# Attention ahead of two MLP layers on one core: the first half's maxima three tiles apart, two weight-conversion steps behind the next first unit, reciprocals ahead of the loads

## The chip, the cores and the metric

The kernel runs on one core of one Trainium2 chip. TensorE (PE; its weight loads are PEld) multiplies, VectorE (DVE), ScalarE (ACT) and GpSimd (POOL) do the elementwise work, and SyncE (SP) issues most of the DMAs, in the order of the program. The metric is the device time of one execution in microseconds (us); less is better.

## The reference

```python
def _attn_ref(q, k, v):                 # 4 x 8 heads, 1152 x 64
    q_pool = q.reshape(B, H, S // 2, 2, D).mean(axis=3)
    scores = scale * np.matmul(q_pool, k.transpose(0, 1, 3, 2))
    scores = scores - np.max(scores, axis=-1, keepdims=True)
    attn = np.exp(scores)
    attn = attn / (np.sum(attn, axis=-1, keepdims=True) + 1e-09)
    return np.matmul(attn, v)
# x: 2304 tokens x 512; then h = x @ w_in (2048 wide), g = h - tanh(h), x = g @ w_out,
# and the same again with g = h * sigmoid(1.702 h) and other weights.
```

## The kernel before

**Pairs and halves.** Attention takes the 32 heads two at a time, as 16 pairs; a pair has 576 pooled queries and is worked off in two halves of 288 queries. The loop `for h in range(NH)` runs over the 32 halves; even halves are a pair's first, odd ones its second. The program writes every engine's order out by hand (`todo[h]`, and the lists filled by `at(h, place, job)` and run by `do(h, place)`); no scheduler moves anything.

**What a half holds.** Nine score tiles S (`scores`, line 429: three matmul steps with high and low parts of q and k, and a fourth that adds the row of negated maxima, `row`), each followed by an exponential on ACT (L435). Between them stand "units" X (`unit`, L359, L351 for unit 6, called R here) that compute the maxima of the *next* pair, each ended by a DVE reduction (L371) out of PSUM, and in even halves the two "corner" units C (L366) of the pair itself. Then come the products with v (`products`, L480) and the sums over ones (L493). In an even half the order is given by `usual[0]`, in an odd one by `usual[1]`, where units 4 to 8 of the next pair stand; unit 4 is the first non-S of an odd half.

**PSUM.** All of these tiles come from one pool of four buffers, handed out in turn: a tile can start when the reader of the tile four before it is done.

**The row of maxima.** When unit 6 (R) of the next pair is reduced, `max_rows` and `send_rows(p + 1, 0)` put the maxima into a row with six small DMAs of SP (L388, `row<-tt`). The first S of the next even half needs that row in its fourth step.

**The sums' way.** `sums` (SP, L514) sends the sums of the pair before to DVE's layout, `recip` adds and inverts them (DVE L522, L523) and writes them to DRAM (SP, L525, `rd<-r`), `spread` reads them back broadcast (SP, L531, `rbd<-rd`), and `normalise` multiplies (DVE, L540). `recip` stands at the end of the even half, `spread` at the start of the odd one; on SP, `spread` stands ahead of the six row DMAs.

**Weights of the first layer** are converted along the way, each piece over four halves: `shift` (ACT L142 and DVE L143), `sign` (DVE L149), `flush` (DVE L156), `tail` (DVE L163), then `split` (ACT L170, POOL L171). `shift` and `flush` stand at the end of an even half, ahead of `recip`.

**Loads.** By their shapes `load_k` and `load_v` move 576 KB each, `load_sum` and `fetch_low` 288 KB each, and the two of `spread` 288 KB together. `load_k` (L290) is the first thing on SP in an even half, ahead of `sums`; `load_v` (L294) and `load_sum` (L285) stand in the place "load", after the last unit. `fetch_low` (L342, `ql<-qd`) is the first thing on SP in an odd half.

**POOL** adds the first probabilities of a half (L446), three in a row and one more after a DVE addition (`rest`, L464), and computes `kl` (L328), which is told to wait for the last DVE instruction noted in `last["v"]` (`recip`'s or `normalise`'s).

Of the kernel before, what the change touches and what calls it, by code (L numbers as in the profile page):

```python
# [7 lines left out]
F32 = mybir.dt.float32  # L8
F32R = mybir.dt.float32r
I32 = mybir.dt.int32  # L10
AF = mybir.ActivationFunctionType
# [12 lines left out]
def f32(ap):  # L24
    return ap.bitcast(F32)
# [3 lines left out]
def tile_pooled_attention_two_moe(  # L29
# [11 lines left out]
    nc = tc.nc  # L41
# [92 lines left out]
    def convert_steps(raw, hi, lo, shape, box, eng=None):  # L134
        def shift():
            box["t"] = wpool.tile([128, DM], I32, tag="wt", name="wt", bufs=2)
            if raw.dtype == F32:
                nc.scalar.activation(f32(box["t"][:]), raw, AF.Copy)
                return
            top = raw[:, :, 1]  # L140
            box["a"] = wpool.tile([128, DM], F32, tag="wa", name="wa", bufs=1)
            nc.scalar.activation(box["a"], f32(top), AF.Abs)  # L142
            nc.vector.tensor_scalar(  # L143
                out=box["t"], in0=top, scalar1=3, scalar2=0x3FFFFFF8,
                op0=ALU.logical_shift_left, op1=ALU.bitwise_and,
            )

        def sign():
            nc.vector.scalar_tensor_tensor(  # L149
                out=box["t"], in0=raw[:, :, 1], scalar=-0x40000000, in1=box["t"],  # L150
                op0=ALU.bitwise_and, op1=ALU.bitwise_or,
            )

        def flush():
            t, a = box["t"], box["a"]
            nc.vector.scalar_tensor_tensor(  # L156
                out=f32(t[:]), in0=a, scalar=2.0 ** -15 * 1.125, in1=f32(t[:]),
                op0=ALU.is_ge, op1=ALU.mult,
            )

        def tail():
            t = box["t"]
            nc.vector.scalar_tensor_tensor(  # L163
                out=t, in0=raw[:, :, 0], scalar=29, in1=t,
                op0=ALU.logical_shift_right, op1=ALU.bitwise_or,
            )

        def split():
            t = f32(box["t"][:]).rearrange("p (a b) -> p a b", a=shape)
            nc.scalar.activation(hi, t, AF.Copy)  # L170
            job = (eng or nc.gpsimd).tensor_tensor(lo, t, f32(hi), op=ALU.subtract)  # L171
            if eng is None:
                after(job, last.pop("rest", None))

        def nothing():
            pass

        bits = [sign, flush, tail] if raw.dtype == I32 else [nothing] * 3
        return [shift, *bits, split]

# [38 lines left out]
    def attention(ctx: ExitStack):  # L219
# [124 lines left out]
        def unit(p, n):  # L344
            d = pairs[p]
            mx = ps.tile([128, 2, 512], F32, tag="ps", name="mx")
            a = n - 9
            if n == 6:
                for j in range(4):
                    for s, r in enumerate(sides):  # L350
                        nc.tensor.matmul(  # L351
                            mx[:, s, KN * j:KN * j + KN], d["qh"][r, 128 * j:128 * j + 128],
                            d["kh"][r, 2 * 512:], start=True, stop=True)
                out = d["mt"][:, 20:28].rearrange("p (j s) -> p j s", j=4)
                src = mx.rearrange("p s (j k) -> p j s k", j=4)
            elif n < 9:
                j, c = divmod(n if n < 6 else n - 1, 2)
                for s, r in enumerate(sides):
                    nc.tensor.matmul(  # L359
                        mx[:, s, :], d["qh"][r, 128 * j:128 * j + 128],  # L360
                        d["kh"][r, 512 * c:512 * c + 512], start=True, stop=True)
                out, src = d["mt"][:, 10 * c + 2 * j:10 * c + 2 * j + 2], mx
            else:
                for h in range(2):
                    for s, r in enumerate(sides):
                        nc.tensor.matmul(  # L366
                            mx[:, s, 0:HB], d["cq"][r, (1 - h) * QL:(3 - h) * QL],
                            d["kh"][r, h * SP + a * HB:h * SP + a * HB + HB],
                            start=(h == 0), stop=(h == 1))
                out, src = d["mt"][:, 8 + 10 * a:10 + 10 * a], mx[:, :, 0:HB]  # L370
            nc.vector.tensor_reduce(out, src, AX.X, ALU.max, negate=True)  # L371
# [174 lines left out]
        def at(h, when, fn, *args):  # L546
            jobs.setdefault((h, when), []).append(lambda: fn(*args))
# [2 lines left out]
            for job in jobs.pop((h, when), ()):  # L550
                job()

        usual = "S C S C S S X S S S X S S X X", "S X S S S X S R S S S X S X"
        begin = "S X S S S X S C S S S C S X X", "S X S S S X S S X S X S S R X X"
        NH = 2 * NPAIR
        todo, ahead = {}, {}
# [19 lines left out]
        for n, (kind, f) in enumerate(order):  # L576
            ld, shift, *more, split = piece(kind, f)
            mine = slots_at[4 * n:4 * n + 4]
            at(mine[0] - 1, "load", ld)
            at(mine[0], "pre" if mine[0] % 2 else "end", shift)  # L580
            for h, job in zip(mine[1:], more, strict=True):
                at(*((h, "end") if h < NH - 2 else (NH - 1, "pre")), job)
            at(mine[-1] + 1, "pre" if mine[-1] + 1 < NH - 1 else "end", split)
        for c in range(NKC):
            at(NH - 2, "pre", split_high, 0, c)
# [2 lines left out]
        for p in range(NPAIR):  # L588
            h = 2 * p
            if p > 0:  # L590
                at(h - 2, "load", load_v, p)
                if p == 1:
                    at(h - 2, "pre", prep_corner, p)
                    at(h - 2, "end", prep_ql, p)
                    at(h - 2, "pool", prep_kl, p, 0)
                    at(h - 1, "end", prep_kl, p, 1, nc.vector)
                else:
                    at(h - 2, "pool", prep_kl, p, 0)
                    at(h - 1, "pool", prep_kl, p, 1)
                    at(h - 1, "first", fetch_low, p, "ql")  # L600
                at(h, "start", sums, p - 1)
                at(h, "pre" if h == NH - 2 else "end", recip, p - 1)
                at(h + 1, "start", spread, p - 1)
                at(h + 1, "end", normalise, p - 1)
            if p > 1:
                at(h - 4, "start", new_pair, p)
                at(max(h - 6, 0), "start", load_one, p)
                at(max(h - 6, 0), "gp" if p > 2 else "start", load_other, p)
                at(h - 4, "load", load_sum, p)
                at(h - 4, "first", load_k, p)  # L610
                at(h - 3, "pre", prep_qh, p)
                at(h - 3, "pre", prep_corner, p)
                at(h - 3, "pre", minus_qh, p)
                at(h - 3, "pre", prep_kh, p, 0)
                at(h - 3, "pre", prep_kh, p, 1)
                at(h - 3, "gp", take_qh, p)
# [51 lines left out]
        for h in range(NH):  # L668
            p, x = divmod(h, 2)
            do(h, "first")  # L670
            do(h, "start")
            g = h * KT
            t = 0
            late = [t for g in rest_of(p, x) for t in g[1:]] if h < NH - 1 else []
            for u in todo[h]:
                if u is None:
                    scores(g + t)
                    if h < NH - 1 and t < KADD - full(p, x) or t < 4:
                        add(p, x, t)
                    elif h == NH - 1 and t in (5, 7):  # L680
                        add_two(p, x, t)
                    t += 1
                    if t == KT and late and h != 1:
                        add_rest(p, x, late.pop(0))
                    continue
                unit(*u)
                if u == (p + 1, 6):
                    max_rows(p + 1, 0)
                    send_rows(p + 1, 0)
                if u == (p, 10):  # L690
                    max_rows(p, 1)
                    send_rows(p, 1)
                if t == KT and late:
                    add_rest(p, x, late.pop(0))
                    if late and x == 0 and full(p, x):
                        add_rest(p, x, late.pop(0))
                        end_rows(p)
            while late:
                add_rest(p, x, late.pop(0))
            if h == NH - 2:  # L700
                end_rows(p)
            do(h, "load")
            do(h, "pre")
            do(h, "gp")
            products(p, x)
            if x == 0 and not full(p, x):
                end_rows(p)
            do(h, "end")
            do(h, "pool")
# [652 lines left out]
```

## Time and profile before

| | us |
|---|---|
| median of three runs | 1176.01 |
| the three runs | 1171.54, 1176.01, 1176.41 |
| the profiled execution, own time | 1176.05 |
| its span in the profile | 1174.3 |
| attention in the span | about 0 to 392 |
| PE busy / DVE busy / ACT busy / POOL busy | 1161.6 / 992.5 / 652.9 / 453.6 |

The span is that of the trace; the execution's own time has 1.75 us more around it. PE counts as busy from a matmul's modelled start to its end, so a share of 99% does not say that PE is never held up; that is read from the chain and from the distances between equal pieces of work.

### The profile page before, as it was taken

Reading aid. Unit: us, or ns where it says so; the run is one execution under the profiler, and the core shown is the slowest. Engines: PE = TensorE matmul, PEld = TensorE weight load, DVE = VectorE, ACT = ScalarE, POOL = GpSimd, SP = SyncE. Lnnn points to the kernel's source line nnn. Section 1 sums busy time; section 2 is a strip of 40 time slices with the busy share of each in tenths; the row PEclk is TensorE's granted clock in tenths of the full one; section 3 lists DMA queues with packets and bytes.
Section 4 is the critical chain, followed back from the end, with each engine's and each line's share of the span. In section 5 each row is a group of like instructions: output and inputs, shape, how many; then the busy total and the mean of one; then the engine's idle time right before and its main releaser. Section 6 shows DMA issues by size and latency. Waiting matters only on the chain.

```text
span 1174.3 us, 23203 instructions
## 1 busy us (share of the span) xinstructions
PE 1161.6 (99%) x9260; PEld 971.5 (83%) x9260; DVE 992.5 (85%) x1242; ACT 652.9 (56%) x969; POOL 453.6 (39%) x321
## 2 busy tenths in 40 slices
PE   9999999999999999999999999999999999999998
PEld 7767676767777888888898898898889999999996
DVE  6888988878988799999999999998986899886442
ACT  4667566656665678676666666655654333342220
POOL 7667676766766223333232333221000222222211
PEclk9999999999999999999999999999999999999999
DMA  6455655555542021111111111112998757765512
GB/s 191 123 118 137 162 127 133 146 143 130 125 111 62 12 64 36 55 54 37 54 36 54 37 36 36 37 54 95 389 389 311 275 215 287 269 225 206 206 54 90
DMA packets 58221, 156.29 MB, mean 133 GB/s; under 512 B 14080, under 2 KB 19712, under 8 KB 58112
## 3 DMA queue, kind: packets, MB, share of 16 engines
q1 hardware_dynamic: 53536, 146.14, 35.8%
q0 software_dynamic: 4032, 8.26, 4.9%
q8 instruction: 73, 1.20, 0.4%
q10 hardware_dynamic: 544, 0.39, 0.1%
q14 instruction: 36, 0.29, 0.1%
HBM read 124.39 MB, written 33.69 MB: 135 GB/s over the span
## 4 chain that ended last, share of the span: by engine, by line
PE 77%; DVE 14%; ACT 4%; issue 2%; DMA 1%; POOL 1%; SPq 1%; DVEq 0%; ACTq 0%; POOLq 0%
PE sc L429 13%; PE y L1048 13%; PE y L1236 12%; PE h L1139 11%; PE acc L480 11%; PE b L996 5%; PE a L996 3%; PE c L996 3%; PE mx L359 3%; DVE work L1182 2%; DVE work L1199 2%; DVE wt L149 2%; DVE wt L143 1%; ACT work L1180 1%; PE acc L493 1%
## 5 line engine op out<-in xcount | busy, mean ns | idle before, releaser
L371 DVE TENSOR_REDUCE mt<-mx 128x2 fp32r<-128x1024 f32 (+2 forms) x176 | 198.1, 1136 | 41.0 <-PE mx L359 22.1
L435 ACT ACTIVATE pf<-sc 128x576 f32<-128x576 f32 x288 | 173.8, 655 | 24.2 <-PE sc L429 15.1
L1236 PE MATMUL y<-mem,big 128*128 128x512 f32 (+1 forms) x780 | 185.1, 368 | 1.2 <-POOL mem L1153 1.2
L1236 PEld LDWEIGHTS y<-mem,big 128*128 128x128 f32 x780 | 142.6, 188 | 21.2 <-POOL mem L1153 2.3
L1034 POOL TENSOR_TENSOR mem<-work,mem 128x768 fp32r<-128x768 f32 x24 | 46.2, 1938 | 289.4 <-ACT mem L1029 274.4
L446 POOL TENSOR_TENSOR sum<-sum,pf 128x576 f32<-128x576 f32 x95 | 137.4, 1446 | 29.2 <-DVE rest L464 23.9
L480 PE MATMUL acc<-pf,v 128*32 128x288 f32 x2304 | 146.3, 407 | 0.0
L1139 PE MATMUL h<-mem,big 128*128 128x512 f32 (+1 forms) x564 | 127.1, 377 | 0.0
L480 PEld LDWEIGHTS acc<-pf,v 128*32 128x32 f32 x2304 | 71.6, 110 | 65.6 <-ACT pf L435 5.0
L1139 PEld LDWEIGHTS h<-mem,big 128*128 128x128 f32 x564 | 104.4, 188 | 17.0
L1153 POOL TENSOR_TENSOR mem<-work,mem 128x1024 fp32r<-128x1024 f32 (+1 forms) x40 | 89.1, 2227 | 75.9 <-ACT mem L1151 75.9
L1048 PE MATMUL y<-big,mem 128*128 128x512 f32 x405 | 114.0, 390 | 0.0
L1201 ACT ACTIVATE work<-work 128x1024 f32<-128x1024 f32 (+1 forms) x40 | 39.1, 977 | 107.5 <-DVE work L1199 107.5
L429 PE MATMUL sc<-qh,kh 64*128 64x288 f32 x576 | 94.0, 315 | 0.0
L171 POOL TENSOR_TENSOR big<-wt,big 128x512 fp32r<-128x512 f32 x25 | 32.6, 1302 | 155.5 <-ACT big L170 142.5
L429 PE MATMUL sc<-row,sel 64*128 64x288 f32 x576 | 88.5, 293 | 3.9 <-DMA row<-tt 2.4
L1048 PEld LDWEIGHTS y<-big,mem 128*128 128x128 f32 x405 | 76.0, 188 | 15.5
L429 PE MATMUL sc<-qh,kl 64*128 64x288 f32 x576 | 87.5, 293 | 0.0
L429 PE MATMUL sc<-ql,kh 64*128 64x288 f32 x576 | 87.2, 292 | 0.0
L1139 PE MATMUL h<-mem,w 128*128 128x512 f32 (+1 forms) x376 | 84.7, 377 | 0.0
L501 ACT ACTIVATE u<-acc 128x576 f32<-128x576 f32 x30 | 19.6, 653 | 107.3 <-PE acc L493 107.3
L1139 PEld LDWEIGHTS h<-mem,w 128*128 128x128 f32 x376 | 69.6, 188 | 11.3
(176 smaller groups left out, 2580.5 us busy)
## 6 DMA issues: line engine op xcount, KB each, us to landing
mem<-x SPq DMA_DIRECT2D x36, 768.0 KB
big<-x SPq DMA_DIRECT2D x27, 768.0 KB
raw<-in_moe_w_in_dram SPq DMA_DIRECT2D x32, 512.0 KB
raw<-in_moe_w_out_dram SPq DMA_DIRECT2D x32, 512.0 KB
v<-in_v_dram SPq DMA_DIRECT2D x16, 576.0 KB
x<-big SPq DMA_DIRECT2D x12, 768.0 KB
kr<-in_k_dram SPq DMA_DIRECT2D x15, 576.0 KB
rbd<-rd SPq DMA_DIRECT2D x32, 144.0 KB
```

The costliest lines, as they stand in the source:

```text
L371: nc.vector.tensor_reduce(out, src, AX.X, ALU.max, negate=True)
L429: nc.tensor.matmul(sc[:, s, 0:HB], w[r], m[r, xs], start=(n == 0), stop=(n == 3))
L435: nc.scalar.activation(pf, sc[:, :, 0:HB], AF.Exp, scale=SCALE)
L446: job = nc.gpsimd.tensor_add(out, parts[p, x], new)
L480: nc.tensor.matmul(acc[32 * n:32 * n + 32, 0], pairs[p]["v"][:, s, t, 32 * h:32 * h + 32], new[t][:, s, :], start=(t == 0), stop=(t == KT ...
L996: nc.tensor.matmul(bank[nm][:, fp, 0:G], w[:, wo, a, 128 * c:128 * c + 128], x[:, b, c, :], start=(k == 0), stop=(k == 5))
L1034: eng.tensor_tensor(g[:, :, 1], halves[n][:, fp], f32(g[:, :, 0]), op=ALU.subtract)
L1048: nc.tensor.matmul(y, gts[2 * side + fp][:, j, r, 128 * t:128 * t + 128], wo[:, p, :], start=(k == 0), stop=(k == len(terms) - 1))
L1139: nc.tensor.matmul(hb[:, j, 0:TBS[b]], wi[:, c, w, :], x[r][c], start=(k == 0), stop=(k == 3 * NKC - 1))
L1153: eng.tensor_tensor(gt[:, :, 1, :], g, f32(gt[:, :, 0, :]), op=ALU.subtract)
L1201: nc.scalar.activation(a, u, AF.Relu, bias=-T2)
L1236: nc.tensor.matmul(ys[m][:, 0:w], lhsT, rhs, start=(fp == 0 and not low and j == p == 0), stop=(fp == 1 and low and j == 1))
```

## The change

The two C units of an even half stand together behind the first S, and the X units come after 3, 6 and 9 score tiles (and one more) where they came after 4, 7 and 9. `shift` and `flush` move from the end of an even half to a new place "mid" in the odd half after it, just behind unit 4 and its reduction; ACT's `Abs` moves from `shift` to `sign`, which stands at the end of an odd half. `recip`, with its SP write, moves from the end of an even half to a new place "rows", behind `end_rows`, which is between the reductions of the last two X units and, on SP, ahead of the loads. `load_k` moves from the head of the even half to the place "load".

```diff
         def shift():
             ...
-            box["a"] = wpool.tile([128, DM], F32, tag="wa", name="wa", bufs=1)
-            nc.scalar.activation(box["a"], f32(top), AF.Abs)
             nc.vector.tensor_scalar(...)
         def sign():
+            box["a"] = wpool.tile([128, DM], F32, tag="wa", name="wa", bufs=1)
+            nc.scalar.activation(box["a"], f32(raw[:, :, 1]), AF.Abs)
             nc.vector.scalar_tensor_tensor(...)
...
-        usual = "S C S C S S X S S S X S S X X", "S X S S S X S R S S S X S X"
+        usual = "S C C S S X S S S X S S S X X", "S X S S S X S R S S S X S X"
...
-            at(mine[0], "pre" if mine[0] % 2 else "end", shift)
+            at(*((mine[0], "end") if mine[0] == NH - 2 else (mine[0] + 1, "mid")), shift)
             for h, job in zip(mine[1:], more, strict=True):
-                at(*((h, "end") if h < NH - 2 else (NH - 1, "pre")), job)
+                if h >= NH - 2:
+                    at(NH - 1, "pre", job)
+                elif h % 2:
+                    at(h, "end", job)
+                else:
+                    at(h + 1, "mid", job)
...
-                at(h, "pre" if h == NH - 2 else "end", recip, p - 1)
+                at(h, "pre" if h == NH - 2 else "rows", recip, p - 1)
...
-                at(h - 4, "first", load_k, p)
+                at(h - 4, "load", load_k, p)
...
                 unit(*u)
+                if u == (p + 1, 4):
+                    do(h, "mid")
...
                         end_rows(p)
+                        do(h, "rows")
```

## Rows read from the trace of the kernel before

**Rows 1.** The page, part 1: busy us, share of the span, instructions.
```profile
PE 1161.6 (99%) x9260; PEld 971.5 (83%) x9260; DVE 992.5 (85%) x1242; ACT 652.9 (56%) x969; POOL 453.6 (39%) x321
```
**Rows 2.** Chain in order of time (start, length): first score tiles of odd halves.
```profile
75.03 0.73 PE sc L429 x8
...
99.72 0.73 PE sc L429 x8
...
123.02 0.73 PE sc L429 x8
...
169.49 0.73 PE sc L429 x8
...
193.40 0.73 PE sc L429 x8
...
239.91 0.73 PE sc L429 x8
...
266.75 0.72 PE sc L429 x8
```
**Rows 3.** The same chain, where it runs through a row DMA.
```profile
250.71 2.92 DMA row<-tt
```
**Rows 4.** Windows: busy us by engine, then granted clock, DMA share, GB/s.
```profile
252.00:254.00 2.00, 0.41 (x5) 0.32 (x5) 0.08 (x1) 0.22 (x1) 1.39 (x1) 1.00 0.39 70
254.00:256.00 2.00, 2.00 (x21) 2.00 (x22) 0.76 (x1) 0.87 (x2) 0.00 (x0) 0.53 0.66 194
```
**Rows 5.** SP's queue in order of time (start, length), in three odd halves.
```profile
128.68 3.29 SPq L388 DMA_DIRECT2D row<-tt  x6
...
176.07 3.36 SPq L388 DMA_DIRECT2D row<-tt  x6
...
246.21 2.15 SPq L531 DMA_DIRECT2D rbd<-rd  x2
248.45 3.29 SPq L388 DMA_DIRECT2D row<-tt  x6
```
**Rows 6.** Waits, 60 to 385 us: total us, times, longest.
```profile
SPq L290 <- POOL kl L328: 43.7, 12, 4.6
SPq L531 <- DMA rd<-r: 32.8, 14, 4.6
...
PEld mx L359 <- DVE mt L371: 4.8, 13, 0.4
```
**Rows 7.** DVE in order of time, an even half into the next odd.
```profile
158.83 1.56 DVE L371 TENSOR_REDUCE mt<-mx 128x2 fp32r<-128x576 f32 x2 [0.46 <-PE mx L366]
...
163.87 1.41 DVE L464 TENSOR_TENSOR rest<-pf 128x576 f32<-128x576 f32 x1
...
168.43 1.21 DVE L371 TENSOR_REDUCE mt<-mx 128x2 fp32r<-128x1024 f32 x1
169.56 0.68 DVE L156 SCALAR_TENSOR_TENSOR wt<-wa,wt 128x512 f32<-128x512 f32 x1
170.16 0.18 DVE L522 TENSOR_REDUCE r<-s 128x9 f32<-128x27 f32 x1
170.37 0.22 DVE L523 RECIPROCAL r<-r 128x9 f32<-128x9 f32 x1
170.50 1.22 DVE L371 TENSOR_REDUCE mt<-mx 128x2 fp32r<-128x1024 f32 x1
172.31 2.36 DVE L371 TENSOR_REDUCE mt<-mx 128x2 fp32r<-128x1024 f32 x2 [0.59 <-PE mx L359]
```
**Rows 8.** POOL in order of time, three places.
```profile
163.24 1.42 POOL L446 TENSOR_TENSOR sum<-sum,pf 128x576 f32<-128x576 f32 x1
...
192.35 1.27 POOL L171 TENSOR_TENSOR w<-wt,w 128x512 fp32r<-128x512 f32 x1 [1.62 <-DVE rest L464]
...
269.14 1.43 POOL L446 TENSOR_TENSOR sum<-pf 128x576 f32<-128x576 f32 x1 [0.43 <-ACT pf L435]
```
**Rows 9.** DVE's reduction of unit 4 in the half of the last row above.
```profile
267.76 1.23 DVE L371 TENSOR_REDUCE mt<-mx 128x2 fp32r<-128x1024 f32 x1 [0.56 <-PE mx L359]
```

## The prediction

> **What bounds the kernel now.** I read the page first, then the chain, then the queues that feed it. PE is busy for 1161.6 of 1174.3 us [rows 1], so the reader is to see that only time in which PE is held up can be won, and that the change touches attention alone, which ends at about 392 us.
>
> The chain in order of time shows how regular attention is. From the first score tile of an odd half to that of the next is 23.30 us in an undisturbed pair (99.72 to 123.02). Three pairs are longer: 75.03 to 99.72 is 24.69, 169.49 to 193.40 is 23.91, 239.91 to 266.75 is 26.84 [rows 2]. Against 23.30 these are 1.39, 0.61 and 3.54 us, 5.54 us together. In the longest one the chain goes through a row DMA of 2.92 us that starts at 250.71 [rows 3]: the first score tile of the even half stands with its fourth step until the row has landed. PE is then busy for 0.41 of the two us from 252 to 254, and the granted clock in the next two is 0.53, which is mostly the lower of the two levels, 1.2 GHz [rows 4]. So of the 3.54 us a part is the wait and the rest the slow matmuls after it; both go if the row is there in time.
>
> SP's queue shows why the row was late. The six issues take 3.3 us and begin at 128.68 in an undisturbed pair, 5.66 us after its odd half began at 123.02. They begin at 176.07, 6.58 us after the half's start at 169.49, and at 248.45, 8.54 us after 239.91; in the last the two `spread` DMAs stand directly ahead, from 246.21 for 2.15 us [rows 2, 5]. `spread` waits for `rd` to land: 32.8 us over 14 halves, 4.6 at the longest [rows 6]. The row DMAs wait behind it in the queue though they need nothing of it.
>
> **The change part by part.**
>
> *Reciprocals ahead of the loads.* `recip` (0.18 and 0.22 us) runs from 170.16 to 170.59 now, behind X4's predecessor X3 (168.43) and a conversion step (169.56) [rows 7]. Put ahead of X3's reduction it ends about 1.9 us earlier, and its write goes out ahead of 576 + 288 + 576 KB of loads instead of behind 864 KB of them. So `rd` lands at least 1.9 us earlier and `spread` should be through before the row is ready. The late starts are 0.92 and 2.88 us over the undisturbed 5.66, which covers the waits of 0.61 and of the long pair's first part; I take the whole 5.54 us as won. Bounds: 0 (the rows are late for another cause) and 5.54. How this stands to the runs: the profiled execution took 1176.05 us, the median is 1176.01, and the fastest run, 1171.54, would be one in which most of these waits did not come up.
>
> On DVE the same move puts 0.43 us (170.16 to 170.59) ahead of X3's reduction. Its buffer is wanted by the second score tile of the odd half. X3 ends at 168.43 + 1.21 = 169.64; PE gets there after its first tile (169.49 + 0.73) and an X of about 0.2, so at 170.45 [rows 2, 7]. The 0.8 us of slack pay for the 0.43, and must also pay for the part below that makes the first `rest` later by some 0.2 us. What is left is about 0.1 us; I charge 0.05 us in each of 14 pairs, 0.7 us, with 0 and 2 us as bounds.
>
> *The order of the first halves.* Now X3 follows on X1 with three tiles between, so it takes X1's buffer and waits for its reduction: 4.8 us in 13 halves [rows 6], 0.37 each. In the new order X3 takes the buffer of a score tile. Against that, the two C reductions (1.56 us back to back [rows 7]) stand together, a tile of the second C's buffer follows after only two score tiles and an X, and X1 now takes X0's buffer, while X0's reduction can only begin behind both corners, `max_rows` and the transposition. By DVE's durations PE would stand there for 0.1 to 0.25 us. I take 0.1 us per even half as won, 1.4 us over 14; bounds 0 and 4.8.
> The corners being ahead of the second score tile also make that tile's exponential later by one corner's matmuls, and with it POOL's three additions, of which the last now runs from 163.24 to 164.66. DVE's `rest` begins at 163.87 and takes 1.41 us, ending 0.62 us after POOL's addition [rows 7, 8], so it does nothing until POOL is through. That is the 0.2 us charged above.
>
> *Two conversion steps to "mid".* `flush` takes 0.60 us from its start to the next one's (169.56 to 170.16), and DVE stands idle for 0.59 us before the second unit of an odd half, at 172.31 [rows 7]. The step fits into that gap, so I cost it at nothing. What hides it is this gap alone. The point is POOL: the step has two inputs in SBUF, as `rest` has, so it would also wait out a POOL addition. In the half where nothing held POOL back its first addition began at 269.14, having waited for ACT, and X4's reduction ended at 267.76 + 1.23 = 268.99 [rows 8, 9]. The step starts at that end and so comes 0.15 us ahead of the addition. In the six halves in which `split` runs on POOL just before, `kl` may still be running then; the step there is the shorter `shift`, and I expect at most 0.2 us, against which `Abs` no longer delays these halves' exponentials. Both are left at nothing.
>
> *`Abs` with `sign`* goes to ACT at the start of an even half, in front of the exponentials. There its 0.6 us come up beside the wait on the corners, not on top of it: nothing.
>
> *`load_k`* waits on SP for POOL's `kl`, 43.7 us in 12 halves [rows 6], with `sums` and the corner rows behind it. At its new place that wait is gone and these go earlier, off the path. It is issued most of a half later; ACT converts the data behind the last unit of the odd half. What comes behind `rd` is then 576 + 288 + 576 KB, 288 of `ql` and 288 of `spread`: 2.0 MB. At 194 GB/s for a share of 0.66 [rows 4], 294 GB/s in full, that is an estimated 6.9 us. Begun about 1 us into the half it is over at 8; the last row DMA is issued at 9. Nothing, but without much room.
>
> Sum: 1176.05 - 5.5 - 1.4 + 0.7 = 1169.85, so **1169.9 us**.
>
> **A rule to weigh.** The Trainium skill, GPSIMD Engine Reference, section 8 (Key points), says that POOL shares its SBUF interfaces with DVE and contends with DVE instructions that have two SBUF inputs or run in a two-port mode. `rest` above shows the first, by this trace. Whether RECIPROCAL is of the second kind no row shows, and the page VectorE: DVE Perf Modes, "The perf-mode tier table", does not list it. By the rule the sum would become that of rival 2.
>
> **The rivals.**
>
> 1. *The rows stay late.* The six issues are no longer behind a waiting `spread`, but their packets are behind 2.0 MB of loads, of which `load_k` is new at this place. For it: the small room above. Against: in the undisturbed pair they had 5.66 us too and caused no wait. If all is kept the time is 1176.05 - 0.7 = 1175.4; if half, 1172.6.
>
> 2. *The reciprocal stands behind POOL.* In six even halves `split` starts on POOL right behind the last `rest` (192.35, 1.27 us [rows 8]), which is where `recip` now comes. Nowhere in this trace do the two overlap. If DVE's reciprocal waits as `rest` did, X3's reduction comes some 1.2 us later, the slack of 0.1 is gone and PE stands for 1.1 to 1.2 us: 6 x 1.2 = 7 us, so 1177.
>
> 3. *"mid" loses to POOL (the other side).* If POOL's first addition of the odd half begins before X4's reduction ends, the step waits for the addition's 1.43 us [rows 8] and the next unit's reduction comes 1.3 us late; its buffer is wanted four tiles on, with some 0.1 us to spare. That is 1.2 us in 14 halves, 17 us, so 1187. It decides from an addition that starts 0.15 us earlier than 269.14 does against 268.99 on. Against it: the addition waits for ACT, not for `kl`, so an earlier `recip` does not bring it forward.
>
> 4. *The order gains in full.* If the corners cost nothing, 4.8 instead of 1.4 are won, and 1166.5 comes out.
>
> **How the numbers follow.** Forecast, 1168 to 1171.5: 0.52. Rival 1: 0.18. Rival 2: 0.10. Rival 3: 0.08. Rival 4: 0.12. 0.5% of 1176.01 is 5.9 us, about what a measurement of this kernel can tell from no change; the line is at 1170.1 below and 1181.9 above. A little over half of the forecast's chance lies below 1170.1 (0.29), all of rival 4 too: faster 0.41. Rival 3 and some 0.02 for mishaps: slower 0.10. The rest, 0.49, within 0.5%. The range takes in rivals 4, 1 and 2 and leaves out rival 3: 1166.5 to 1177.5.
>
> **What would show it.** Right: the six row issues begin 5.6 to 5.8 us into every odd half; no pair over 23.4 us after the first; no stretch with the granted clock at 1.2 GHz inside attention; `rd` ahead of `v` on SP. Order: X3 no longer waits on DVE, and even halves are about 0.1 us shorter. Rival 2: RECIPROCAL over 0.3 us in halves with L171. Rival 3: the steps L143 and L156 at 1.5 to 2 us behind X4, and PE idle before the sixth tile of odd halves. Wrong it would also be if the three long pairs were the luck of one execution and the runs compared have fewer of them.

## The result, and the profile after

The changed kernel takes 1183.18 us, the median of six runs (1178.98 to 1184.23). The kernel before took 1174.78 in the runs beside it. The ratio is 1.007, with an interval of 1.0047 to 1.0092: slower by 0.7%, and above the predicted range.

| profiled execution | before | after |
|---|---|---|
| own time, us | 1176.05 | 1184.20 |
| span, us | 1174.3 | 1182.4 |
| attention, from the first score tile of half 3 to that of half 31 | 330.0 | 338.3 |

So attention, 8.3 us longer, holds all of the difference. The page of the changed kernel, part 1, shows 14.8 us more on DVE than [rows 1]:

```profile
PE 1162.9 (98%) x9260; PEld 970.6 (82%) x9260; DVE 1007.3 (85%) x1242; ACT 652.9 (55%) x969; POOL 455.2 (38%) x321
```

**Long odd halves.** The length of a half is counted here from its first score tile to that of the next half. Undisturbed odd halves take 11.5 to 11.7 us. Five of them (7, 11, 15, 19, 23) take 13.0 instead. PE's timeline shows the first steps of halves 7 and 8:

```profile
101.49 0.40 PE L429 MATMUL sc<-qh,kh 64*128 64x288 f32 x2
...
114.54 0.40 PE L429 MATMUL sc<-qh,kh 64*128 64x288 f32 x2
```

That is 13.05 us; the same half of the kernel before took 11.61. DVE's timeline and then POOL's, same half, show what lies in it:

```profile
101.03 0.22 DVE L523 RECIPROCAL r<-r 128x9 f32<-128x9 f32 x1
101.16 1.16 DVE L371 TENSOR_REDUCE mt<-mx 128x2 fp32r<-128x1024 f32 x1
102.57 1.22 DVE L371 TENSOR_REDUCE mt<-mx 128x2 fp32r<-128x1024 f32 x1 [0.24 <-PE mx L359]
103.71 2.33 DVE L141 TENSOR_SCALAR wt<-raw 128x512 int32<-128x512 int32 x1
105.96 2.34 DVE L371 TENSOR_REDUCE mt<-mx 128x2 fp32r<-128x1024 f32 x2
```
```profile
100.85 1.28 POOL L171 TENSOR_TENSOR w<-wt,w 128x512 fp32r<-128x512 f32 x1 [1.62 <-DVE rest L464]
102.07 0.85 POOL L281 DMA_DIRECT2D qd<-in_q_dram  x1
102.65 1.71 POOL L328 TENSOR_TENSOR kl<-kr,kh 128x576 fp32r<-128x576 f32 x1
104.08 1.66 POOL L446 TENSOR_TENSOR sum<-pf 128x576 f32<-128x576 f32 x1
105.82 1.47 POOL L446 TENSOR_TENSOR sum<-sum,pf 128x576 f32<-128x576 f32 x1
```

`shift` (L141 here, L143 before) stands behind unit 4's reduction at 103.71 and ends at 106.04. POOL is in `kl` when it starts, and goes on into the first addition; `shift` ends 0.3 us after that addition. The next unit's reduction starts 3.39 us behind unit 4's (105.96 against 102.57), and PE waits for it (the row `PE sc L429 <- DVE mt L371` further down has five waits). The reciprocal at 101.03 takes 0.22 us although `split` (L171) runs on POOL from 100.85 to 102.13. The five halves in which this happens are those with `split` and also `load_other`'s DMA (L281) on POOL ahead of `kl`; half 27 has no `load_other`, and takes 11.6 us.

**Rows still late, for another cause.** The waits of SP's queue and of PE, 60 to 385 us, first one row of the kernel before that [rows 6] leaves out, then those of the changed kernel:

```profile
SPq L525 <- DVE r L523: 51.4, 13, 6.7
```
```profile
SPq L525 <- DVE r L523: 69.4, 13, 6.1
...
SPq L388 <- DMA kr<-in_k_dram: 5.9, 6, 1.5
SPq L531 <- DMA rd<-r: 5.1, 7, 1.3
SPq L388 <- DMA ql<-qd: 3.2, 9, 0.7
SPq L388 <- DMA qs<-qd: 0.8, 1, 0.8
...
SPq L290 <- POOL kl L328: 0.6, 4, 0.2
```
```profile
PE sc L429 <- DVE mt L371: 6.0, 5, 1.2
PE sc L429 <- DMA row<-tt: 3.0, 3, 1.7
```

`spread` waits 5.1 us for `rd` instead of 32.8, as meant, and the wait for `kl` is all but gone (0.6 us instead of 43.7). But the row DMAs (L388) now wait for *loads* to land, which none did before. Half 5, which begins at 76.01, shows it in SP's timeline, from the even half before it on; below it the same loads in the kernel before, where half 5 begins at 75.03:

```profile
67.85 1.14 SPq L388 DMA_DIRECT2D row<-tt  x2
69.03 1.03 SPq L388 DMA_DIRECT2D cr<-tt  x2
75.80 0.33 SPq L525 DMA_DIRECT2D rd<-r  x1
76.23 0.38 SPq L294 DMA_DIRECT2D v<-in_v_dram  x1
76.74 0.35 SPq L285 DMA_DIRECT2D qs<-qd  x1
77.19 0.37 SPq L290 DMA_DIRECT2D kr<-in_k_dram  x1
78.09 0.33 SPq L342 DMA_DIRECT2D ql<-qd  x1
79.17 1.14 SPq L531 DMA_DIRECT2D rbd<-rd  x2
81.90 5.53 SPq L388 DMA_DIRECT2D row<-tt  x6
```
```profile
72.30 0.37 SPq L294 DMA_DIRECT2D v<-in_v_dram  x1
73.19 0.33 SPq L285 DMA_DIRECT2D qs<-qd  x1
76.16 0.33 SPq L525 DMA_DIRECT2D rd<-r  x1
```

The six issues take 5.53 us instead of 3.29 [rows 5]. Counting back along the queue, the fourth row DMA is the eighth behind `qs`, the fifth behind `kr`, the sixth behind `ql`; and these three are what the waits name. So in this program a DMA of SP is issued only when the one eight places ahead of it has landed. The other thing to see is the hole from 70.06 to 75.80: SP waits for the reciprocal (L525, 69.4 us in all), and the three loads behind it go out into the odd half. SP waited for the reciprocal in the kernel before, too (51.4 us), but with the loads already issued.

In four even halves (4, 6, 22, 24) the row then comes late, for 6.0 us together by the lengths of the halves (0.4, 2.2, 2.1, 1.3). In the kernel before it was 5.8 in three: [rows 2] give 5.5, but two of those three pairs are of the kind of halves 9 and 10, which take 23.17 us together, and not of that of 7 and 8, with 23.30. How far the row is late follows from the issues: they stretch by 2.24 us in half 5 (5.53 against 3.29) and half 6 is 2.2 us longer; in half 23, below, they stretch by 1.30 and half 24 is 1.3 us longer. In half 21 it is 1.7 for 2.1.

```profile
302.65 4.59 SPq L388 DMA_DIRECT2D row<-tt  x6
```

The lengths account for the difference: five halves by 1.4 us are 7.0; rows 6.0 - 5.8 = 0.2; all else in attention, taken from executions with neither, is 1.0 (taken up under the reasons). Sum 8.2 of 8.3.

### The profile page after: what moved, and what is told of

The parts are those of the page before. It is cut to its first block, busy times and chain, and to the rows that moved or that the text cites. A ratio compares the mean times of both kernels' runs of the same rounds, so it can differ in the third digit from the quotient of the medians.

```text
span 1182.4 us, 23216 instructions
## 1 busy us (share of the span) xinstructions
PE 1162.9 (98%) x9260; PEld 970.6 (82%) x9260; DVE 1007.3 (85%) x1242; ACT 652.9 (55%) x969; POOL 455.2 (38%) x321
## 4 chain that ended last, share of the span: by engine, by line
PE 37%; DVE 20%; ACT 6%; issue 2%; POOL 0%; DVEq 0%; ACTq 0%
PE y L1056 12%; PE y L1244 7%; PE h L1147 6%; PE b L1004 5%; PE a L1004 3%; PE c L1004 3%; DVE work L1207 3%; DVE work L1190 3%; DVE wt L149 2%; ACT work L1188 2%; DVE wt L141 2%; DVE xb L1264 2%; DVE wt L156 2%; ACT work L1209 2%; DVE wt L163 1%
## 5 line engine op out<-in xcount | busy, mean ns | idle before, releaser
L371 DVE TENSOR_REDUCE mt<-mx 128x2 fp32r<-128x1024 f32 (+2 forms) x176 | 195.7, 1128 | 36.1 <-PE mx L359 18.8
L429 PE MATMUL sc<-qh,kh 64*128 64x288 f32 x576 | 94.2, 320 | 6.5 <-DVE mt L371 6.0
L429 PE MATMUL sc<-row,sel 64*128 64x288 f32 x576 | 87.7, 293 | 5.2 <-DMA row<-tt 3.0
L171 POOL TENSOR_TENSOR big<-wt,big 128x512 fp32r<-128x512 f32 x25 | 32.5, 1300 | 155.5 <-ACT big L170 150.6
L429 PE MATMUL sc<-qh,kl 64*128 64x288 f32 x576 | 85.8, 292 | 0.0
L429 PE MATMUL sc<-ql,kh 64*128 64x288 f32 x576 | 85.7, 291 | 0.0
L429 PEld LDWEIGHTS sc<-qh,kh 64*128 64x128 f32 x576 | 54.8, 184 | 28.8 <-DVE mt L371 12.3
```

The source lines that it names most:

```text
L429: nc.tensor.matmul(sc[:, s, 0:HB], w[r], m[r, xs], start=(n == 0), stop=(n == 3))
```

## The experiments

Each kernel is the changed one with the edit shown, unless said otherwise. Ratios are to the kernel before, whose median differed a little from group to group (1172.87 to 1174.72), because its row waits differ from one execution to the next.

**e1_mid_back, e2_loadk_back, e3_both_back: parts undone.** e1 puts both conversion steps back, e2 `load_k`, e3 both.

```diff
# e1
-            at(*((mine[0], "end") if mine[0] == NH - 2 else (mine[0] + 1, "mid")), shift)
+            at(mine[0], "pre" if mine[0] % 2 else "end", shift)
...
# e2
-                at(h - 4, "load", load_k, p)
+                at(h - 4, "first", load_k, p)
```

> The changed kernel with shift and flush back at the end of the even half (the place mid is empty); reciprocals, order, load_k and Abs as changed. Theory 1 (the step at mid stands behind POOL): the five odd halves of 13.0 us go back to about 11.6, 5 x 1.44 = 7.2 us less than the changed kernel's 1183.2, so 1176; the waits for the row stay, some 5 us in all. Theory 2 (the loss is the late row alone): 1183, and the long odd halves stay.

> The changed kernel with load_k back at the head of the even half. Theory 1 (a row DMA waits on SP until the load issued eight DMAs before it has landed; with load_k out of the way the loads land sooner and the eighth before is another): the row DMAs are issued without gaps, the waits for the row of the even halves 4, 6, 22 and 24 (5.5 us) go, so 1177.5; the five odd halves of 13.0 us stay. Rival (the row is late because its reduction R is late, in the long odd halves): the waits stay with the long halves, 1182 to 1183.

> Both undone: what stays of the change is the order of the first halves, the reciprocals ahead of the loads, and Abs with sign. Theory 1: 7.2 and 5.5 us less than 1183.2, so 1170.5, which is the forecast for the whole change; no odd half over 11.7, no pair over 23.4. Rival (the order of the first halves costs too): 1173 or more, with even halves over 11.75.

| | us | ratio |
|---|---|---|
| e1 | 1201.10 | 1.0234 (1.0216 to 1.0253) |
| e2 | 1178.37 | 1.0036 (1.0014 to 1.0057) |
| e3 | 1200.52 | 1.0229 (1.0211 to 1.0247) |

e2 came out as expected, 0.9 us above the figure: no row waits for a load, and the five halves of 13.0 us stay. e1 and e3 went the other way by 25 to 30 us, and the theory that "mid" was simply the wrong place fell. DVE's and POOL's timelines of e1, half 6 into 7:

```profile
101.61 0.21 DVE L523 RECIPROCAL r<-r 128x9 f32<-128x9 f32 x1
...
102.82 3.77 DVE L141 TENSOR_SCALAR wt<-raw 128x512 int32<-128x512 int32 x1
```
```profile
102.65 0.85 POOL L281 DMA_DIRECT2D qd<-in_q_dram  x1
103.23 1.72 POOL L328 TENSOR_TENSOR kl<-kr,kh 128x576 fp32r<-128x576 f32 x1
104.65 1.64 POOL L446 TENSOR_TENSOR sum<-pf 128x576 f32<-128x576 f32 x1
```

`shift` now lasts 3.77 us and PE stands for 3 us. By the program `kl` waits for the DVE instruction noted in `last["v"]`, the reciprocal. Before, the reciprocal stood *behind* the step and so held `kl` back until the step was done; brought forward, it lets `kl` go first. That was a reading only, and e8 tests it.

**e8_both_back_hold: that reading, by itself.** e3, and the two steps note themselves in `last["v"]`, so that `kl` waits for them.

```diff
-            nc.vector.tensor_scalar(
+            last["v"] = nc.vector.tensor_scalar(
                 out=box["t"], in0=top, scalar1=3, scalar2=0x3FFFFFF8,
...                                      # the same in flush; and e3's two edits
```

> The kernel e3_both_back (1200.5) with one more edit: shift and flush, at the end of the even half, note themselves in last["v"], so that kl waits for them as it did before the change. Theory C (e1 and e3 lost because recip, now early, releases kl, and kl takes POOL's side ahead of the conversion step): kl starts behind the step again, the odd halves go from 12.0 and 16.2 to 11.5, and the time is 1171. Rival (the step at the end is late for another cause, the reciprocal ahead of X3): 1190 or more.

1171.82 us, 0.9999 (0.9988 to 1.0009): 28.7 us below e3 by these dependences alone, so the order between `kl` and the step is the cause of the loss in e1 and e3. DVE's and POOL's timelines of e8, half 6 into 7:

```profile
99.28 0.42 DVE L141 TENSOR_SCALAR wt<-raw 128x512 int32<-128x512 int32 x1
```
```profile
99.11 0.85 POOL L281 DMA_DIRECT2D qd<-in_q_dram  x1
99.83 1.58 POOL L328 TENSOR_TENSOR kl<-kr,kh 128x576 fp32r<-128x576 f32 x1
```

The step is through before `kl` starts, and it takes its 0.42 us although POOL is issuing the DMA meanwhile.

**e4_pool_order: "mid" kept, POOL's order changed.** `load_other` issues its DMA ahead of `split`, so that `kl` follows on `split` at once.

```diff
-                at(max(h - 6, 0), "gp" if p > 2 else "start", load_other, p)
+                at(max(h - 6, 0), "load" if p > 2 else "start", load_other, p)
```

> The changed kernel with load_other issued by POOL ahead of the split instead of behind it; shift and flush stay at mid. Theory 1a (kl is late because POOL issues the DMA for 0.85 us between split and kl; the step then finds kl still running and loses its turn to the addition as well): kl ends about 2.0 us into the odd half as it does in half 27, the step runs in 0.42 us, the five long halves become 11.6, so 1176. Theory 1b (at mid the step loses to POOL's additions whatever kl does): 1183, L141 over 2 us.

DVE's timeline of e4, half 7, and the waits of its row DMAs:

```profile
105.22 0.42 DVE L141 TENSOR_SCALAR wt<-raw 128x512 int32<-128x512 int32 x1
```
```profile
SPq L388 <- DMA kr<-in_k_dram: 7.5, 11, 1.5
SPq L388 <- DMA ql<-qd: 5.3, 12, 1.8
```

The step takes 0.42 us and the long halves are gone (11.65 at most), so `kl` and what delays it are their cause. But the time is 1182.40 (1.0067, 1.0041 to 1.0093): the row DMAs wait more (14.4 us with two smaller rows of the view, against 9.9), and five even halves (6, 8, 12, 16, 20) are late by 1.3 to 4.7 us, 12.3 together. Four of them come behind a half that was long before; there the six issues begin 1.4 us earlier in the half, and the loads mostly do not. So the long halves had hidden a part of the late rows. That does not cover half 6, the latest: the half ahead of it was never long, and its issues stretch by 2.9 us for 4.7. The rest of it is not explained.

**e5, e6, e7: load_k elsewhere, on top of e4.** e5 issues it by ACT, at the same place of the program; e6 at its old place; e7 in the even half behind `sums`.

```diff
# e5
-            return nc.sync.dma_start(out=kraw[p][:, x], in_=k[p // NPB, p % NPB][:, x])
+            return (nc.scalar if p > 1 else nc.sync).dma_start(
+                out=kraw[p][:, x], in_=k[p // NPB, p % NPB][:, x])
...
# e6
-                at(h - 4, "load", load_k, p)
+                at(h - 4, "first", load_k, p)
...
# e7: "later" is behind "start" in the loop
-                at(h - 4, "load", load_k, p)
+                at(h - 4, "later", load_k, p)
```

> The kernel e4_pool_order with one more edit: load_k is issued at the same place by ACT instead of SP, so the same bytes move at the same time but k is no longer one of SP's eight DMAs in flight. Theory A (a row DMA waits on SP for the DMA issued eight earlier to land): the waits of row<-tt for kr go; the waits for the row in even halves of e4 (about 11 us with the slow clock) shrink to under 2 us in all, and the time is 1172 to 1174. Theory B (the row's packets are late because of the traffic itself): the waits stay, 1181 to 1183.

> The changed kernel with both repairs: load_other ahead of the split (e4) and load_k back at the head of the even half (e2); order, reciprocals and mid as changed. Theory: the two losses are separate and add up; no long odd half and no row gap, 1183.2 - 7.2 - 5.3 = 1170.7. Rival (repairing one brings back the other, since the odd halves get shorter and the row is wanted 1.4 us sooner): 1175 or more.

> load_other ahead of the split, and load_k on SP behind sums and load_one of the even half, where kl is over: sums are not held up and k lands in the even half. Theory: as e6_pool_k_back or a little better, 1170; SP shows no wait of load_k for kl and no wait of row<-tt for a load. Rival (k so early takes the DMA engines from the corner rows): even halves over 11.8, 1173.

1170.97, 1171.29 and 1170.94 us: 0.9986 (0.9975 to 0.9997), 0.9988 (0.9975 to 1.0001) and 0.9988 (0.9978 to 0.9998). No row waits for a load in any of them, but for 0.2 us once in e6. e5 was meant to tell issue from packets, and does not: ACT does not stand behind the write, so `kr` goes out 6.3 to 6.5 us into the even half, where SP in e4 issued it 0.1 to 1.3 us into the odd one. The bytes moved earlier, too. That the rows were late at their issue is read from the stretched issues above, not from e5.

**e12_k_alone: the kernel before, with `load_k` alone moved.** The edit is e2's, the other way round, in the kernel before.

> The kernel before, and in it only load_k moved to the place behind the last unit. Theory (SP's issues wait for the loads issued eight DMAs earlier): the fourth to sixth row DMAs wait for loads in most odd halves and the row comes late in the even ones: 3 to 8 us slower than before, 1176 to 1181. Prediction's costing: nothing, or a little less than before because sums no longer waits behind kl: 1172 to 1173.

1171.88 us, 0.9989 (0.9978 to 1.0001): not slower. The expectation failed, and with it the reading that `load_k`'s place by itself is the cause. SP's timeline, same stretch as above:

```profile
70.64 0.35 SPq L290 DMA_DIRECT2D kr<-in_k_dram  x1
75.90 0.33 SPq L525 DMA_DIRECT2D rd<-r  x1
```

`kr` goes out at 70.64, in the even half, and not at 77.19 in the odd one: no write waits ahead of it.

**e13_rd_behind, e16_pool_rd_behind: the write behind the loads.** The reciprocal stays early on DVE; only its write on SP goes behind the loads. e16 has e4's edit as well.

```diff
         def recip(p):
             ...
-            nc.sync.dma_start(out=rd, in_=r9)
...
+                at(h, "gp", write, p - 1)     # the write alone
```

> The changed kernel, and in it only SP's write of the reciprocals moved behind the loads of the even half; the reciprocal itself stays early on DVE, load_k stays at its new place. Theory: the write is what holds v, qs and kr back until 11.4 us into the even half; with it behind them they go out from 6 us on, the row DMAs wait for no load, the row gaps go and the five halves of 13.0 us stay: 1177.5 to 1179. Rival: load_k's place by itself makes the rows late, and nothing changes: 1182 to 1184.

> The same write behind the loads, in the kernel with load_other ahead of split on POOL (1182.40 us). Theory: both causes are gone and nothing else is, so it is as fast as the versions with load_k moved or on another queue: 1170.5 to 1172. Rival, as above: 1182.

1177.82 us (1.0029, 1.0018 to 1.0041) and 1171.04 (0.9973, 0.9959 to 0.9986), both as the theory had it. The late rows need both: `load_k` at its new place without the early write does no harm (e12, e13), and neither does the early write with `load_k` out from behind it (e2, e5 to e7).

**e9, e10, e11: the order of the first halves, on top of e7.** e9 has the old order; e10 a third one with the corners' row work behind X0; e11 that order with the row work where it was.

```diff
-        usual = "S C C S S X S S S X S S S X X", "S X S S S X S R S S S X S X"
+        usual = "S C S C S S X S S S X S S X X", "S X S S S X S R S S S X S X"   # e9
+        usual = "S C S C S X S S S X S S S X X", "S X S S S X S R S S S X S X"   # e10, e11
...
-                if u == (p, 10):                        # e10 alone
+                if u == (p + 1, 0) and h or h in (0, NH - 2) and u == (p, 10):
                     max_rows(p, 1)
                     send_rows(p, 1)
```

> The repaired version with load_k behind the sums (1170.94 us), and in it only the old order of the first halves, with the corners one tile apart and X units after 4, 7 and 9 tiles. The prediction's term: the new order wins 0.1 us in each of 14 even halves, so the old one gives 1170.9 + 1.4 = 1172.3. What the traces say: even halves of 11.63 and 11.76 us with the new order against 11.69 with the old one, so the order is worth nothing: 1170.4 to 1171.4, with X3's wait on DVE of about 0.38 us back.

> The same repaired version with a third order: corners one tile apart, X units after 3, 6 and 9 tiles and one more, and the corner rows (their reduction, the transposition and SP's issues) behind X0's reduction and no longer ahead of it. Theory: the new order only moved X3's wait to X1 and to the tiles behind the corners, because X0's reduction stood behind both corners and the row work; without that, even halves come out at 11.4 to 11.5 us, 0.2 to 0.3 less in each of 14, so 1167 to 1168. Rival: the even halves are set by ACT's exponentials or by the sums at their end, whatever the order: 1170.5 to 1171.5.

> The third order alone, with the corner rows where they were, ahead of X0's reduction. If DVE's row work ahead of X0 is what made X1 wait, X1 still waits 0.1 to 0.25 us and the time is 1169.5 to 1171. If the waits came from the two corners in a row, it is as fast as the version with the rows behind X0, 1167 to 1168.

e9 1172.00 (0.9992, 0.9983 to 1.0002), e10 1168.63 (0.996, 0.9948 to 0.9971), e11 1169.80 (0.9971, 0.996 to 0.9982). PE's waits before its weight loads, 60 to 385 us, one fence for each of e9, e7, e11:

```profile
PEld mx L359 <- DVE mt L371: 4.8, 13, 0.4
...
PEld sc L429 <- ACT pf L435: 2.3, 7, 0.3
```
```profile
PEld sc L429 <- DVE mt L371: 3.0, 12, 0.3
PEld sc L429 <- ACT pf L435: 2.2, 7, 0.3
```
```profile
PEld mx L359 <- DVE mt L371: 1.5, 6, 0.3
```

With the old order X3 waits 4.8 us for DVE, as in [rows 6]; with the new one score tiles wait 3.0; with the third and the row work ahead of X0 it is 1.5, and with the row work behind X0 (e10) the view has no wait on DVE. The expectation that the order is worth nothing was wrong: e7 is 1.1 us faster than e9. In all four of these kernels (e7, e9, e10, e11) another wait stays, for ACT's exponential, 2.2 or 2.3 us in seven places.

**e14_abs_back, e15_abs_idle: `Abs`, on top of e10.** e14 puts it back at the end of the even half, e15 ahead of the odd half's products.

```diff
         def sign():
-            box["a"] = wpool.tile(...)
-            nc.scalar.activation(box["a"], f32(raw[:, :, 1]), AF.Abs)
...
+                at(mine[0], "end", soon[kind, f])       # e14: Abs alone
+                at(mine[1], "gp", soon[kind, f])        # e15
```

> The third order with the rows behind X0 (1168.63 us), and in it only Abs back at the end of an even half. Theory: at its new place Abs stands ahead of the exponentials of seven even halves and costs 0.3 us in each (11.75 against 11.45), at the old one 0.1 in an odd half: 1.5 us less, 1167.0 to 1167.4. Rival: the longer even halves come from the steps at mid or from split, and Abs costs nothing: 1168.3 to 1169.

> The same, but Abs ahead of the odd half's products, where ACT stands idle for 1.9 us before the copy of the sums. Theory: no exponential waits for it, even halves 11.45 and odd ones 11.53 throughout: 2.2 us less, 1166.2 to 1166.7. Rival: 1168.3 to 1169.

1166.96 us (0.994, 0.9927 to 0.9953) and 1166.64 (0.9934, 0.9921 to 0.9946). ACT's timeline in e10 and in e15, the same half 15 into 16:

```profile
201.58 0.65 ACT L501 ACTIVATE u<-acc 128x576 f32<-128x576 f32 x1 [0.58 <-PE acc L493]
202.13 0.66 ACT L148 ACTIVATE wa<-raw 128x512 f32<-128x512 f32 x1
202.69 1.18 ACT L435 ACTIVATE pf<-sc 128x576 f32<-128x576 f32 x2
```
```profile
199.65 0.69 ACT L136 ACTIVATE wa<-raw 128x512 f32<-128x512 f32 x1
201.47 0.65 ACT L508 ACTIVATE u<-acc 128x576 f32<-128x576 f32 x1 [1.13 <-PE acc L500]
202.19 0.65 ACT L442 ACTIVATE pf<-sc 128x576 f32<-128x576 f32 x1
```

In e10 `Abs` stands between the copy of the sums and the first exponential, which holds the buffer of the fifth tile; the even half takes 11.76 us against 11.44 for one without `Abs`. The seven waits for ACT's exponential are in neither e14's nor e15's view. In e15 it fills idle time and all even halves take 11.44. e15 is the fastest version, 0.66% below the kernel before.

## Why the prediction was wrong

- **"Two conversion steps to mid: nothing, at most 0.2 us" is the step that failed: 7.0 us.** The gap of 0.59 us in [rows 7] and the test of POOL [rows 8, 9] both came from halves without `split` on POOL; in the second `kl` came behind the reciprocal and was over before the addition. The prediction did see that in six halves with `split` the step may meet `kl`, and priced that at 0.2 us from no row. In five of them `split` and `load_other` make `kl` late, and the step stands not for the rest of `kl` alone but for the addition behind it: `shift` lasts 2.3 us instead of 0.42 (e4), and the half is 1.4 us longer.
- **Rival 3 had this mechanism** and a price near it, 1.2 us a half, but put it in all 14 halves, as a loss to the addition; those with `flush` take 11.54 us, so `flush` fits. It was also dismissed with "an earlier `recip` does not bring it forward", without asking what the reciprocal held: e1, e3 and e8 show that the old place of `recip` kept `kl` behind the step, so the two moves could not be priced apart. With the early reciprocal and without "mid" the kernel is 26 us slower than before (e1, e3). The Trainium skill, GPSIMD Engine Reference, section 8 (Key points), names DVE instructions in a two-port mode beside those with two SBUF inputs as ones that contend with POOL. The prediction weighed that for the reciprocal and not for `shift`; `shift` has one SBUF input, and its 2.33 us against 0.42 agree with the rule if it runs in such a mode, which no row here tells.
- **"`load_k`: nothing, but without much room" and "the whole 5.54 us as won" failed together: 6.0 us of late rows in place of 5.8.** Rival 1's outcome came about, but the rows were held at their issue, and not by `load_k`'s place alone (e12). The working counted the 2.0 MB behind `rd` from about 1 us into the odd half. The loads do go out 0.1 to 1.3 us into most of these halves, but `v` and `qs` used to go out in the half before; it did not see that SP stands waiting for the reciprocal with the loads queued behind it (e13), nor that the row DMAs are issued only once a DMA eight ahead has landed.
- **Right:** `spread` no longer blocks the rows' issues, which begin 5.7 to 6.0 us into the undisturbed odd halves (5.6 to 5.8 was predicted) and 7.3 into the long ones. The write of `rd` is 1.2 to 1.6 us earlier, not at least 1.9. Rival 2 is refuted: RECIPROCAL takes 0.22 us beside L171.
- **The order, 1.4 us, was right in size:** e9 against e7 gives 1.1. X3's waits of 4.8 us go and waits of score tiles of 3.0 us come, as the working had it. By the lengths of the halves the new order wins 0.14 us in a pair with `Abs` in its even half (23.56 to 23.42) and 0.08 in one without (23.23 to 23.16), and loses 0.2 in half 30. That the corners' row work ahead of X0 costs as much again is shown by e11 against e10, 1.2 us.
- **"`Abs`: nothing" was mis-sized.** It costs 1.7 us in the third order (e10 against e14). In the order of the change the seven even halves with `Abs` take 11.77 us against 11.63 for those without, 1.0 us together, and in the old order 12.05 against 11.70 (e9), 2.5 together; these two are comparisons of halves, and no run took `Abs` alone out of these orders. What is left over is this: attention without late rows takes 324.2 us in the kernel before (330.0 - 5.8; e12, less one late row of 0.2, gives the same), 326.4 with the old order and the rest of the change (e9), 325.2 with the new order (e5 to e7, e16). What "mid" and the reciprocals cost singly was not measured. So the change without its two faults is only 0.1 to 0.3% faster than the kernel before, and in e6 the interval takes in no change.
- **The baseline's waits vary.** The runs of before that were taken beside e5 to e8 go from 1170.15 to 1177.94. The profiled execution of 1176.05 was one with many waits, as the last sentence of the prediction allowed; without its 5.8 us it would have taken an estimated 1170.3. Against medians of 1172.9 to 1174.8 that leaves 2.6 to 4.5 us to be won, and not 5.5.

## What to carry to other kernels

A step that is moved forward on one engine also moves whatever waits for it: list who is released earlier, and who is now queued behind its wait, before its own microseconds are counted. Look for the cover of a moved step in each kind of half, not in the half that happens to be shown. And put a DMA that waits for a computation behind those that wait for nothing, even if it is the more urgent one.

## What the runs showed of the hardware

- A DVE `TENSOR_SCALAR` of 128x512 int32, with one SBUF input, took 0.42 us where POOL stood idle at its start (e4) or was only issuing a DMA (e8). Where POOL was in `kl` and then ran an addition it took 2.33 us and ended 0.3 us behind the addition, so it lost its turn to POOL's next operation, too. In e1 it took 3.77 us, from 0.4 us ahead of `kl` by the trace to 0.3 behind the addition. RECIPROCAL on 128x9 (0.22 us) and TENSOR_REDUCE out of PSUM (1.16 us beside `split`, 1.22 beside `kl`; 1.21 to 1.23 in [rows 7, 9]) stood beside POOL's work without delay.
- SP's issues of the row DMAs waited for the landing of the DMA eight issues earlier (9.9 us in 16 waits); with `load_k` issued by ACT, or early enough, such waits for loads came to 0.2 us at most.
